# Query products as one block of 64x64 quarters behind the second stage's first product, and block sums over alternate tiles

## The chip, the cores and the metric

The kernel runs on one core of one Trainium2 chip. The metric is the device time of one launch in microseconds (us). A core has TensorE for matrix products (PE in the profile; PEld is its loading of weights), VectorE (DVE), ScalarE (ACT), GpSimd (POOL) and SyncE (SP), each of which works through its own instructions in program order and waits on the others' semaphores; DMA queues move data beside them.

## The reference

Linear attention over 8 batches, 8 heads, 576 tokens and head size 64, then an MLP with a residual over the 512 joined features:

```python
q_s = softmax(q, over the 64 features)      # exp, divided by its sum
k_s = softmax(k, over the 576 tokens)
kv  = einsum('bhsd,bhse->bhde', k_s, v)     # one 64x64 matrix a head
x   = einsum('bhsd,bhde->bhse', q_s, kv)    # joined to [8, 576, 512]
xn  = (x - mean) / sqrt(var + 1e-6) * g_ln
out = x + maximum(xn @ w_ch1, 0) @ w_ch2    # 512 -> 2048 -> 512
```

## The kernel before

The first 512 tokens of each batch are four tiles of 128 tokens. They make one turn of the MLP, and the last 64 tokens of all eight batches make a ninth turn of the same size (the code's `C9`, turn 8 when they are counted from 0, as here). Turns 2 to 8 are alike; turns 0 and 1 are special. Turn c runs the MLP of its tokens while the attention of turn c+1 and the loads and exponentials of turn c+2 are woven in between.

**The order.** Nothing schedules itself here. `mlp_steps(c)` gives a list of matmuls, the main line, each with a weight; a 256-column matmul weighs 0.5. A turn's list is 112 long: 0 to 56 is the first stage (features 512 to 2048), 56 to 112 the second (2048 to 512). `run` goes through that list and emits each side item when the sum of the weights reaches its number. So a side item such as `(10, reduce_q)` says where in every engine's program order it stands, and an engine does its instructions in that order, even when a later one could start.

**Both stages have seven products instead of eight** (2x2 blocks, sums of blocks as operands). Their order is 1, 5, 6, 2, 7, 3, 4. In the first stage the work is done for groups 0 and 1 and then, 28 further on, for groups 2 and 3; these are called pair A and pair B here. In each pair, every product is four matmuls of 256 columns for one group and four for the other. With two groups of a pair as g and g':

- products 1, 6, 7 and 4 pile up in one bank of PSUM, `bx`; 5 and 3 in `bb`; 2 in `bc`.
- after product 6 VectorE adds `bx` and a copy of product 5 into `bb` (`add_5`, L773), for g and then for g'. Product 7 adds to the same `bx`, so TensorE starts it for a group only when that group's L773 has read `bx`. Product 3 adds to `bb`.
- after product 7 VectorE writes one quarter of the hidden layer from `bx` (`out_22`, L776), for g and g', and applies the maximum to both (L781). Product 4 adds to `bx` again, so it waits for that group's L776.
- ScalarE copies (L766, L770) and writes the other quarters through the maximum (L784).

The second stage takes sums of the hidden layer's blocks (`sum_h`, L572: four sums over each half of the hidden layer, VectorE), which are side items at 30, 33 and 41 for the first half; its fourth sum and those of the second half come at the second stage's first products. Its products lie in the banks `ba`, `bb`, `bc` and `be` (L589), and VectorE makes the output from them (L601).

**Attention of the next turn.** `reduce_q` (L218) sums the exponentials of q in two instructions of two tiles; `recip_q` (L858) inverts the sums. `kv_pairs` (L361) makes the kv matrices; for each pair of heads `kv_sb` holds a 128x128 matrix with two 64x64 blocks and zeros beside them. `po_mm` (L404) multiplies: 16 matmuls of 128 columns a turn, woven in one by one, four of them to a tile. `x_fast` (L449) scales the tile's result, with its sum, and `xn_out` (L429) centres it. `xn_T` (L267) transposes two tiles by DMA, issued by SP. `sum_x` (L259) takes four differences of blocks of the transposed tiles on GpSimd, each in two instructions; products 5, 6, 7 and 4 of the next turn read them. For the ninth turn `po_mm` has a form of its own (L395): 64x64 quarters, 32 in one block, because the halves of a tile belong to two batches.

**PSUM.** `att_ps` has two banks (kv and query products), `mm_ps` six (the products of both stages).

In before, turn c+1's two `reduce_q` stand at 81 and 91 of turn c-1 and `recip_q` at 2 of turn c; for turn 3 alone the sums stand at 4 and 12 of turn 2. The query products of turn c+1 stand at 13 to 24, 48 to 53, 57 to 59 and 65 to 67 of turn c.

Of the kernel before, what the change touches and what calls it, by code (L numbers as in the profile page):

```python
# [20 lines left out]
def kernel(  # L21
# [16 lines left out]
    nc = tc.nc  # L38
# [66 lines left out]
    def main_src(x, b, h0, hn):  # L105
        return x[b, h0 : h0 + hn, 0:SM, :].rearrange("h (p t) d -> p h (t d)", t=T)

    raws = {}
# [134 lines left out]

    def sum_x(c, i):

        if i == 0:
            tqs[c] = mlp.tile([P, 4, 2, 2, P], BF16, tag="tq", name="tq", bufs=1)
        (b11, b12), (b21, b22) = [
            [xnTs[c][:, 2 * half : 2 * half + 2, 2 * kh : 2 * kh + 2, :] for half in range(2)]
            for kh in range(2)  # L250
        ]
# [130 lines left out]
    pobox = {}  # L382

    def po_mm(c, t, i):


        if c == C9:
            if i == 0 and t % 2 == 0:
                pobox["q"] = [
                    att_ps.tile([P, 2, NP, D], FP32, tag="a", name="po") for _ in range(2)  # L390
                ]
            pobox[c, t] = pobox["q"]
            for m, tok in enumerate(halves):
                for half, hs in enumerate(halves):
                    nc.tensor.matmul(  # L395
                        pobox["q"][half][tok, t % 2, i, :], eqTs[c][hs, t, i, tok],
                        kv_sb[hs, 2 * t + m, i, hs], start=(t % 2 == 0 and i == 0), stop=True,
                        skip_group_check=True,
                    )
            return  # L400
        if i == 0:
            pool, tag = (mm_ps, "m") if c == 0 and t >= 2 else (att_ps, "a")
            pobox["p"] = pobox[c, t] = pool.tile([P, DM], FP32, tag=tag, name="po")
        nc.tensor.matmul(  # L404
            pobox["p"][:, i * P : i * P + P], eqTs[c][:, t, i, :], kv_sb[:, c, i, :],
            start=True, stop=True,
        )
# [25 lines left out]

    def x_fast(c, t):

        x, st, _, mv = xs[c]
        if c == C9:
            for half in range(2):
                nc.vector.scalar_tensor_tensor(
                    x[:, t].rearrange("p (i two d) -> p i two d", two=2, d=D)[:, :, half],  # L440
                    in0=pobox[c, t][half][:, t % 2], scalar=1.0,
                    in1=eqs[c][2][:, t].rearrange("p (i two) -> p i two", two=2)[:, :, half]
                    .to_broadcast([P, NP, D]),
                    op0=ALU.mult, op1=ALU.mult, accum_out=st[:, t, half : half + 1],
                )
            nc.vector.tensor_add(mv[:, t, 0:1], st[:, t, 0:1], st[:, t, 1:2])
            xn_out(c, t)
            return
        nc.vector.scalar_tensor_tensor(  # L449
            x[:, t].rearrange("p (h d) -> p h d", h=H),  # L450
            in0=pobox[c, t].rearrange("p (h d) -> p h d", h=H), scalar=1.0,
            in1=eqs[c][2][:, t].to_broadcast([P, H, D]), op0=ALU.mult, op1=ALU.mult,
            accum_out=mv[:, t, 0:1] if c else st[:, t, 0:1],
        )
        if c:
            xn_out(c, t)
# [163 lines left out]
    def last_products(product):  # L620
# [7 lines left out]
        def stt(t, col, src, add=None, c0=0, cn=DH2):  # L628
            cols = slice(DH2 * col, DH2 * col + DH2)
            cs = slice(c0, c0 + cn)  # L630
            add = xs[c][0][:, t, cols] if add is None else add
            nc.vector.scalar_tensor_tensor(
                part(t, col)[:, cs], in0=src[:, cs], scalar=rstds[c][:, t : t + 1],
                in1=add[:, cs], op0=ALU.mult, op1=ALU.add,
            )

        def store(t0, tn, col):
            cols = slice(DH2 * col, DH2 * col + DH2)
            for half, eng in enumerate((nc.sync, nc.scalar)):
                ps = slice(64 * half, 64 * half + 64)  # L640
                to = out[2 * t0 + half : 2 * (t0 + tn) - 1 + half : 2, SM:S, cols]
                eng.dma_start(to.transpose([1, 0, 2]), yl[ps, t0 : t0 + tn, cols])
# [32 lines left out]
    def mm2_fast(c):  # L675
# [30 lines left out]

        def ys(name, col, t0):
            return [lambda t=t: y_quarter(c, t0 + t, col, hbox[name][:, t]) for t in range(2)]

        def sums(*which):  # L710
            return [lambda g=g, i=i: sum_h(g, i) for g, i in which if g or c == FAST or i == 3 or c == B - 1 and i > 1]

        late = c in (FAST, B - 1)
        product(1, "a", first=True, cut=6, at={
# [10 lines left out]
            1: ys("e", 1, 0)[:1], 4: ys("e", 1, 0)[1:],  # L725
            7: ys("b", 1, 2)[:1], 10: ys("b", 1, 2)[1:], 15: ys("a", 0, 2)})
        return steps

    def prod1(n, g, dst, c, q, ko, first):
# [7 lines left out]
        if n in (1, 2, 3):  # L737
            t0, kh = {1: (0, 0), 2: (0, 1), 3: (2, 1)}[n]
            rhs = xnTs[c][:, t0 : t0 + 2, 2 * kh + ko, :]
        else:  # L740
# [108 lines left out]
    def prep_fast(b):  # L849

        s = [(57, lambda: exp_q(b, 0, 4)), (65, lambda: exp_q(b, 2, 4)), (70, lambda: eq_T(b))]
        s += [(81, lambda: reduce_q(b, 0, 2)), (91, lambda: reduce_q(b, 2, 2))]
        s += [(81, lambda: exp_k(b, 0, 4)), (98, lambda: exp_k(b, 2, 4))]
# [6 lines left out]
    def attn_fast(c):  # L860

        s = [(4 + 4 * t, lambda t=t: reduce_q(3, t, 2)) for t in (0, 2)] if c == 3 else []
        kv, new, ps, squares, ts, rstd = (
            (24, 40, ((48, 53), (57, 59), (65, 67), (73, 75)), (66, 74, 87, 91), (61, 78), 95)
            if c == 3 else
            (3, 10, ((13, 24), (48, 53), (57, 59), (65, 67)), (60, 66, 74, 87), (55, 70), 92)
        )
        s += [(22 if c == 3 else 2, lambda: recip_q(c)), (kv, lambda: kv_pairs(c)), (new, lambda: start_x(c))]
        for t, (p0, p1) in enumerate(ps):
            s += spread([lambda t=t, i=i: po_mm(c, t, i) for i in range(NP)], p0, p1)  # L870
            s += [(p1, lambda t=t: x_fast(c, t)), (squares[t], lambda t=t: square_sum(c, t))]
        s += [(ts[0], lambda: xn_T(c, 0, 2)), (ts[1], lambda: xn_T(c, 2, 2)), (rstd, lambda: rstd_op(c))]
        s += [((84, 100 if c == C9 - 1 else 88, 92, 101)[i], lambda i=i: sum_x(c, i)) for i in range(4)]
        return s

    def second_side():
# [14 lines left out]
        s += [(40, lambda: start_x(2))]  # L891
        for t, (p0, p1) in enumerate(((47, 49), (51, 54), (57, 61), (65, 69))):
            s += spread([lambda t=t, i=i: po_mm(2, t, i) for i in range(NP)], p0, p1)
            s += [(p1, lambda t=t: x_fast(2, t)), ((69, 78, 84, 90)[t], lambda t=t: square_sum(2, t))]
# [3 lines left out]
        s += spread([lambda i=i: sum_x(2, i) for i in range(4)], 95, 108)  # L898
        return s

    def attn_rest():

        s = [(2, lambda: recip_q(C9)), (4, lambda: start_x(C9))]
        for t, (p0, p1, p2) in enumerate(((8, 21, 57), (8, 25, 62), (40, 52, 69), (40, 58, 77))):
            s += [(p0, lambda t=t: [po_mm(C9, t, i) for i in range(NP)])]
            s += [(p1, lambda t=t: x_fast(C9, t)), (p2, lambda t=t: square_sum(C9, t))]
        s += [(27, lambda: xn_T(C9, 0, 2)), (60, lambda: xn_T(C9, 2, 2)), (88, lambda: rstd_op(C9))]
        return s + spread([lambda i=i: sum_x(C9, i) for i in range(4)], 94, 102)

# [172 lines left out]
    with tc.manual_schedule(  # L1082
# [51 lines left out]
        for c in range(1, B):  # L1134
# [3 lines left out]
            else:  # L1138
                if c + 1 < B:
                    side += attn_fast(c + 1)  # L1140
                else:
                    side += attn_rest()
                if c + 2 < B:
# [3 lines left out]
            if c == B - 2:  # L1147
                side += [(1, load_qrem)]
                side += spread([lambda r=r: exp_qrem(r) for r in range(T)], 58, 80)
                side += [(84, lambda: eq_T(C9))]  # L1150
                side += [(84 + 4 * t, lambda t=t: reduce_q(C9, t, 2)) for t in (0, 2)]
            sums = [(53, 0)] if c == FAST else [(p, i) for i, p in enumerate((30, 41) if c == B - 1 else (30, 33, 41))]
            run(mlp_steps(c), side + [(at, lambda i=i: sum_h(0, i)) for at, i in sums])
# [31 lines left out]
```

## Time and profile before

| | before |
|---|---|
| median of 3 runs | 264.61 us (262.91 to 264.71) |
| the profiled execution | 263.19 us |
| its span, first to last instruction | 261.4 us |
| TensorE busy | 255.1 us, 98%, 2667 matmuls |
| VectorE busy | 223.9 us, 86% |
| ScalarE busy | 176.7 us, 68% |
| GpSimd busy | 94.4 us, 36% |
| granted TensorE clock | 0.999 |

The profile is one execution, whose own time lies 1.4 us under the median. TensorE's busy time is the time from a matmul's start to its modelled end, and the matmuls overlap, so the starts tell more than the ends: a 256-column matmul starts 0.109 us after the one ahead of it when nothing holds it up. VectorE's instructions overlap by some 0.08 us as well; what one of them costs the next is the distance between their starts.

### The profile page before, as it was taken

How to read it: one execution, taken by the hardware profiler on the slowest of the kernel's cores; microseconds unless marked ns; L12 is line 12 of the kernel's file. 1: busy time of each engine (PE TensorE's matmuls, PEld its weight loads, DVE VectorE, ACT ScalarE, POOL GpSimd, SP SyncE). 2: the span in 40 equal slices, each digit the busy share in tenths (PEclk: the TensorE clock that was granted, in tenths of full speed). 3: DMA queues.
4: the chain of work that ended last, by engine and by line, in shares of the span. 5: the costliest groups of instructions: out<-in, count | busy, mean ns of one | idle time of the engine just before them, and what ended most of it. 6: DMA issues, size and time to landing. Idle time of an engine off the chain costs nothing.

```text
span 261.4 us, 6802 instructions
## 1 busy us (share of the span) xinstructions
PE 255.1 (98%) x2667; PEld 219.9 (84%) x2667; DVE 223.9 (86%) x505; ACT 176.7 (68%) x348; POOL 94.4 (36%) x148
## 2 busy tenths in 40 slices
PE   8899999999999999999999999999999999999993
PEld 6789755788888998899889889988898888888883
DVE  6778996989999999899889988998898979977873
ACT  4657780997887785789478947894789277538400
POOL 3962228414059205920881088009100800030000
PEclk9999999999999999999999999999999999999999
DMA  7999999989999994999399938995905323221014
GB/s 195 253 206 207 356 215 276 290 192 285 171 143 277 274 174 33 294 264 115 84 263 263 154 79 290 245 153 130 266 4 111 112 102 44 43 104 56 3 41 120
DMA packets 82616, 45.00 MB, mean 172 GB/s; under 512 B 58196, under 2 KB 79192, under 8 KB 82584
## 3 DMA queue, kind: packets, MB, share of 16 engines
q0 software_dynamic: 32464, 21.76, 44.9%
q1 hardware_dynamic: 49488, 22.29, 40.6%
q10 hardware_dynamic: 632, 0.53, 0.7%
q8 instruction: 20, 0.33, 0.5%
q14 instruction: 12, 0.10, 0.1%
HBM read 36.70 MB, written 9.44 MB: 177 GB/s over the span
## 4 chain that ended last, share of the span: by engine, by line
PE 92%; DMA 3%; DVE 2%; SPq 1%; ACT 0%; issue 0%
PE ba L589 21%; PE bx L742 20%; PE bb L742 10%; PE ph L505 8%; PE bb L589 5%; PE bc L589 5%; PE be L589 5%; PE pc L541 5%; PE bc L742 5%; PE po L404 3%; DMA kt<-in_k_dram 3%; PE pkv L361 2%; PE ptr L918 1%; PE pxT L332 1%; SPq L970 1%; DVE bb L773 0%
## 5 line engine op out<-in xcount | busy, mean ns | idle before, releaser
L589 PEld LDWEIGHTS <-hs 128*128 128x128 bf16 x512 | 49.8, 98 | 5.8
L742 PEld LDWEIGHTS <-w_raw 128*128 128x128 bf16 x480 | 45.5, 98 | 5.2
L259 POOL TENSOR_TENSOR tq<-xnT 128x256 bf16<-128x256 bf16 x26 | 16.8, 665 | 73.7 <-DMA xnT<-xn 49.5
L589 PEld LDWEIGHTS <-hT 128*128 128x128 bf16 x392 | 37.4, 98 | 4.2
L742 PEld LDWEIGHTS <-w1g 128*128 128x128 bf16 x360 | 34.3, 98 | 4.3 <-issue 0.3
L742 PE MATMUL bx<-tq,w_raw 128*128 128x256 bf16 x240 | 31.6, 273 | 0.0
L589 PE MATMUL ba<-w_q,hs 128*128 128x256 bf16 x256 | 30.8, 273 | 0.0
L766 ACT COPY bc<-bx 128x512 f32<-128x512 f32 x30 | 16.6, 594 | 19.0 <-PE bx L742 19.0
L773 DVE TENSOR_TENSOR bb<-bx,s 128x512 f32<-128x512 f32 x30 | 19.5, 694 | 8.2 <-ACT s L770 5.5
L607 POOL DMA_DIRECT2D out_dram<-ot x28 | 15.5, 559 | 23.7 <-DVE ot L601 23.6
L784 ACT ACTIVATE hT<-bb 128x512 bf16<-128x512 f32 x30 | 16.3, 595 | 10.8 <-PE bb L742 10.8
L417 ACT ACTIVATE scrap<-x,mv 128x512 bf16<-128x512 bf16 x32 | 23.1, 722 | 0.3
L784 ACT ACTIVATE hT<-bc 128x512 bf16<-128x512 f32 x30 | 16.3, 594 | 8.9 <-PE bc L742 8.9
L572 DVE TENSOR_TENSOR hs<-hT 128x1024 bf16<-128x1024 bf16 x32 | 21.7, 685 | 0.5 <-ACT hT L784 0.5
L404 PE MATMUL po<-kv_sb,eqT 128*128 128x128 bf16 x128 | 22.0, 219 | 0.0
L776 DVE TENSOR_TENSOR hT<-bx,s 128x512 bf16<-128x512 f32 x30 | 19.3, 683 | 3.1 <-PE bx L742 3.1
L449 DVE SCALAR_TENSOR_TENSOR x<-po,rq 128x512 bf16<-128x512 f32 x30 | 20.5, 683 | 0.9 <-PE po L404 0.8
L218 DVE TENSOR_REDUCE zq<-eq 128x16 f32<-128x1024 bf16 (+1 forms) x20 | 20.8, 1050 | 0.5 <-ACT eq L209 0.5
L615 ACT COPY s<-ba 128x512 f32<-128x512 f32 x15 | 8.8, 585 | 14.7 <-PE ba L589 9.7
L784 ACT ACTIVATE hT<-bx 128x512 bf16<-128x512 f32 x30 | 16.4, 602 | 0.7 <-PE bx L742 0.6
L589 PE MATMUL ba<-w_sb,hT 128*128 128x256 bf16 x128 | 16.6, 273 | 0.0
L770 ACT COPY s<-bb 128x512 f32<-128x512 f32 x30 | 16.6, 622 | 0.0
(157 smaller groups left out, 553.5 us busy)
## 6 DMA issues: line engine op xcount, KB each, us to landing
out_dram<-ot POOLq DMA_DIRECT2D x30, 256.0 KB, 6.4
kt<-in_k_dram SPq DMA_DIRECT2D x5, 1024.0 KB, 12.3
qt<-in_q_dram SPq DMA_DIRECT2D x4, 1024.0 KB, 5.9
qt<-in_q_dram POOLq DMA_DIRECT2D x2, 1024.0 KB, 12.5
kt<-in_k_dram POOLq DMA_DIRECT2D x2, 1024.0 KB, 13.7
vm<-in_v_dram POOLq DMA_DIRECT2D x16, 128.0 KB, 11.1
qt<-in_q_dram SPq DMA_DIRECT2D x3, 512.0 KB, 4.7
w_raw<-in_moe_w_ch_dram POOLq DMA_DIRECT2D x3, 512.0 KB, 10.3
```

Of the source, the lines that this page charges most:

```text
L218: nc.vector.reduce_sum(eqs[c][1][:, ts], eqs[c][0][:, ts], axis=AX.X)
L259: eng.tensor_tensor(out=dst[:, t], in0=x[:, t], in1=y[:, t], op=ALU.subtract)
L404: nc.tensor.matmul(pobox["p"][:, i * P : i * P + P], eqTs[c][:, t, i, :], kv_sb[:, c, i, :], start=True, stop=True,)
L417: nc.scalar.activation(scrap, x[:, t], AF.Square, bias=mv[:, t, 0:1], scale=-float(DM), accum_out=mv[:, t, 1:2],)
L449: nc.vector.scalar_tensor_tensor(x[:, t].rearrange("p (h d) -> p h d", h=H), in0=pobox[c, t].rearrange("p (h d) -> p h d", h=H), scalar=1. ...
L505: nc.tensor.matmul(ph[:, m % 2, at : at + tn], (w1g if c else w1_sb)[:, ko, m * P : (m + 1) * P], xnTs[c][:, t0 : t0 + tn, ko, :], start=( ...
L572: nc.vector.tensor_tensor(out=dst, in0=x, in1=y, op=op)
L589: nc.tensor.matmul(hbox[bank][:, t, cs], lhsT, rhs[:, cs], start=first and (own or t == 0) and k == 0, stop=k == KH - 1, skip_group_check= ...
L742: nc.tensor.matmul(dst[:, q], lhsT, rhs, start=first and q == 0 and ko == 0, stop=ko == 1, skip_group_check=True)
L773: nc.vector.tensor_tensor(out=at[g, "b"], in0=at[g, "x"], in1=at[g, "s"], op=ALU.add)
L776: nc.vector.tensor_tensor(out=h_out(g, 1, 1), in0=at[g, "x"], in1=at[g, "s"], op=ALU.add)
L784: nc.scalar.activation(h_out(g, odd, half), at[g, name], AF.Relu)
```

## The change

1. **Query products.** For turns 3 to 8 the 16 woven matmuls become one block (`po_block`) of 64 quarters of 64x64: only the blocks of `kv_sb` that aren't zero are multiplied. It stands at 64, behind the second stage's first product. It writes two banks of `att_ps` for tiles 0 and 1 and two of `mm_ps` for tiles 2 and 3. Turn 8 has it in place of its two blocks of 32.
2. **What reads them.** `x_pair` replaces `x_fast`: for two tiles, four scalings of 256 columns, one add for the two sums, two centrings. Both pairs stand at 64, and so do the two transposes (64.1 and 64.3).
3. **Sums of exponentials.** The two `reduce_q` move from 81 and 91 of the turn before to 10 and 26 of this turn, `recip_q` from 2 to 40.
4. **Alternate tiles.** The halves of the tokens that the seven products work on were tiles 0, 1 and 2, 3; they are now tiles 0, 2 and 1, 3 (not for turns 0 and 1). One instruction of a `sum_x` then needs the first transpose alone and the other the second; the four first ones stand at 84, the four others at 88, all on GpSimd (VectorE did turn 8's eight and two of turn 7's).
5. **Sums of the hidden layer.** The fourth `sum_h` of the first half moves from the second stage (product 6) to 45. Turn 7, which had only two there (30 and 41), gets the same four places.
6. **Turn 1.** Its `x_fast` for tile 0 moves from 49 to 52.6, so behind L776 and L781 of its pair; tile 3's query product moves from 65..69 to 62..65; tiles 2 and 3 take banks of `mm_ps`; `sum_x` stands at 88 and 94.

```diff
+    def paired(c):
+        return c > 1
+    def half_tiles(c, half):
+        return slice(half, T, 2) if paired(c) else slice(2 * half, 2 * half + 2)
...
+    def sum_x(c, i, ts=range(2)):
...
-        eng = nc.vector if c == C9 or (c == C9 - 1 and i == 1) else nc.gpsimd
-        for t in range(2):
-            eng.tensor_tensor(out=dst[:, t], in0=x[:, t], in1=y[:, t], op=ALU.subtract)
+        for t in ts:
+            nc.gpsimd.tensor_tensor(out=dst[:, t], in0=x[:, t], in1=y[:, t], op=ALU.subtract)
...
+    def po_block(c):
+        for t0, pool, tag in ((0, att_ps, "a"), (2, mm_ps, "m")):
+            banks = [pool.tile([P, 2, NP, D], FP32, tag=tag, name="po") for _ in halves]
+            for t in range(2):
+                pobox[c, t0 + t] = [bank[:, t] for bank in banks]
+                for i in range(NP):
+                    for m, tok in enumerate(halves):
+                        for bank, hs in zip(banks, halves):
+                            nc.tensor.matmul(
+                                bank[tok, t, i, :], eqTs[c][hs, t0 + t, i, tok],
+                                kv_sb[hs, 2 * (t0 + t) + m if c == C9 else c, i, hs],
+                                start=(t == 0 and i == 0), stop=True, skip_group_check=True,
+                            )
...
+    def x_pair(c, t0):
+        x, st, _, mv = xs[c]
+        for t in (t0, t0 + 1):
             for half in range(2):
                 nc.vector.scalar_tensor_tensor(
...
+        ts = slice(t0, t0 + 2)
+        nc.vector.tensor_add(mv[:, ts, 0:1], st[:, ts, 0:1], st[:, ts, 1:2])
+        for t in (t0, t0 + 1):
             xn_out(c, t)
...
     def attn_fast(c):
-        s = [(4 + 4 * t, lambda t=t: reduce_q(3, t, 2)) for t in (0, 2)] if c == 3 else []
...
+        s = [(at, lambda t=t: reduce_q(c, t, 2)) for t, at in ((0, 10), (2, 26))]
+        s += [(40, lambda: recip_q(c))]
+        if c < C9:
+            s += [(24 if c == 3 else 3, lambda: kv_pairs(c))]
+        s += [(60, lambda: start_x(c)), (64, lambda: po_block(c))]
+        s += [(64 + p, lambda t=t: x_pair(c, t)) for t, p in ((0, 0), (2, 0.2))]
+        s += [(64.1, lambda: xn_T(c, 0, 2)), (64.3, lambda: xn_T(c, 2, 2))]
+        s += [((72, 76, 80.5, 87)[t], lambda t=t: square_sum(c, t)) for t in range(T)]
+        s += [(92, lambda: rstd_op(c))]
+        s += [(84 + 4 * t, lambda i=i, t=t: sum_x(c, i, (t,))) for t in range(2) for i in range(4)]
...
-            sums = [(53, 0)] if c == FAST else [(p, i) for i, p in enumerate((30, 41) if c == B - 1 else (30, 33, 41))]
+            sums = [(53, 0)] if c == FAST else [(p, i) for i, p in enumerate((30, 33, 41, 45))]
```

More of the change, by code (lines that the diff above doesn't have):

```diff
@@ L382 @@
     pobox = {}
-    def po_mm(c, t, i):
[L387 to L400, printed above, removed]
+    def po_block(c):
[11 more added lines that the diff above has]
+                            )
+    def po_mm(c, t, i):
         if i == 0:
-            pool, tag = (mm_ps, "m") if c == 0 and t >= 2 else (att_ps, "a")
+            pool, tag = (mm_ps, "m") if c in (0, 2) and t >= 2 else (att_ps, "a")
             pobox["p"] = pobox[c, t] = pool.tile([P, DM], FP32, tag=tag, name="po")
@@ L405, in po_mm @@
             pobox["p"][:, i * P : i * P + P], eqTs[c][:, t, i, :], kv_sb[:, c, i, :],
-            start=True, stop=True,
+            start=(i == 0), stop=True, skip_group_check=True,
         )
@@ L705, in mm2_fast, with ys @@
             return steps
-        def ys(name, col, t0):
-            return [lambda t=t: y_quarter(c, t0 + t, col, hbox[name][:, t]) for t in range(2)]
+        def ys(name, col, half):
+            return [
+                lambda t=t: y_quarter(c, tile_of(c, half, t), col, hbox[name][:, t])
+                for t in range(2)
+            ]
         def sums(*which):
-            return [lambda g=g, i=i: sum_h(g, i) for g, i in which if g or c == FAST or i == 3 or c == B - 1 and i > 1]
-        late = c in (FAST, B - 1)
+            return [lambda g=g, i=i: sum_h(g, i) for g, i in which if g or c == FAST]
+        late = c == FAST
         product(1, "a", first=True, cut=6, at={
```

59 lines of the change are left out of this document (18 added, 41 removed).

## The prediction

> **What bounds the kernel.** I read the chain of waits first. It is TensorE from end to end:
>
> ```profile
> PE 92%; DMA 3%; DVE 2%; SPq 1%; ACT 0%; issue 0%
> ```
>
> Then the timeline of TensorE within turn 4, whose first matmul starts at 128.66. All times below that have no trace time beside them count from such a first matmul.
>
> ```profile
> 131.27 1.04 PE L742 MATMUL bx<-tq,w_raw 128*128 128x256 bf16 x8
> 132.14 0.38 PE L742 MATMUL bc<-xnT,w1g 128*128 128x256 bf16 x2
> ...
> 133.13 0.71 PE L742 MATMUL bx<-tq,w_raw 128*128 128x256 bf16 x5
> ```
>
> Eight matmuls take 0.87 (131.27 to 132.14): 0.109 each, with no hole. A turn's 224 make 24.46; with the kv products (0.86 with what they cost at both ends) and 16 query products (0.055 each: 132.36 to 132.42 in the timeline) that is 26.2, which is what a turn takes (129.48 to 155.69 from one turn's kv products to the next's). So from turn 2 on TensorE never waits. The change can win only what it takes from TensorE's stream, and loses whatever wait it brings in. The candidate is VectorE, in the first stage, since TensorE there waits for it four times a pair (L773 and L776, each group). Its timeline in turn 4, where the last number of a row is the idle time ahead of it:
>
> ```profile
> 131.98 1.30 DVE L773 TENSOR_TENSOR bb<-bx,s 128x512 f32<-128x512 f32 x2 [0.63 <-PE bx L742]
> 133.76 1.29 DVE L776 TENSOR_TENSOR hT<-bx,s 128x512 bf16<-128x512 f32 x2 [0.49 <-PE bx L742]
> 135.09 0.43 DVE L781 TENSOR_SCALAR hT<-hT 128x1024 bf16<-128x1024 bf16 x1
> 135.43 0.68 DVE L449 SCALAR_TENSOR_TENSOR x<-po,rq 128x512 bf16<-128x512 f32 x1
> ...
> 138.33 1.30 DVE L773 TENSOR_TENSOR bb<-bx,s 128x512 f32<-128x512 f32 x2 [0.49 <-ACT s L770]
> 139.53 0.68 DVE L572 TENSOR_TENSOR hs<-hT 128x1024 bf16<-128x1024 bf16 x1
> 140.13 1.28 DVE L776 TENSOR_TENSOR hT<-bx,s 128x512 bf16<-128x512 f32 x2
> ```
>
> The pairs run without slack to speak of: the second L773 ends at 133.27 (4.61), and product 7 of that group, the fifth matmul of the row at 133.13, starts at 133.57: 0.30 later. What a late one costs, turn 1 shows (VectorE, then TensorE):
>
> ```profile
> 61.89 1.27 DVE L776 TENSOR_TENSOR hT<-bx,s 128x512 bf16<-128x512 f32 x2
> ```
> ```profile
> 61.81 0.71 PE L742 MATMUL bb<-xnT,w_raw 128*128 128x256 bf16 x5
> 62.62 0.38 PE L742 MATMUL bx<-tq,w1g 128*128 128x256 bf16 x2
> ```
>
> Five matmuls from 61.81 are through at 62.36; product 4 starts at 62.62, 0.05 after the first L776 ends (62.56). So a wait is paid in full, plus 0.05.
>
> **Query products.** The form is in the trace, in turn 7:
>
> ```profile
> 208.16 1.04 PE L742 MATMUL bb<-tq,w_raw 128*128 128x256 bf16 x8
> 209.13 0.45 PE L395 MATMUL po<-kv_sb,eqT 64*64 64x64 bf16 x32
> 209.51 1.05 PE L742 MATMUL bx<-tq,w_raw 128*128 128x256 bf16 x8
> ```
>
> The eight matmuls are through at 209.03, the next start at 209.51: 0.48 for 32 quarters. 0.09 is lost ahead (209.03 to 209.13); by the single starts four quarters follow each other every 0.032, so eight fours are 0.25, and the remaining 0.13 is lost at the first four and behind. A block of 64 pays this once: 16 x 0.032 + 0.22 = 0.72, against 16 x 0.055 = 0.88. That is -0.16 in each of turns 2 to 6 and 2 x 0.48 - 0.72 = -0.24 in turn 7: **-1.0**. Four banks in place of two are not in the trace; bounds are nothing saved and the quarters at a quarter of a whole matmul's time (rival D). The Trainium skill (TensorEngine Tiling, Theoretical Speedup) promises up to 2x for each small dimension, 4x for both; its Key Properties say that a change of tiling mode drains the engine. The 0.09 is that drain. The 4x does not hold here: 0.032 against 0.055 is 1.7x. By 4x the block would be 0.44, and the gain 2.7 in place of 1.0.
>
> **The sums of exponentials.** One `reduce_q` costs VectorE 1.13: in turn 2, where before has one between L773 and L776, it starts at 79.88 and the next at 81.01.
>
> ```profile
> 78.68 1.30 DVE L773 TENSOR_TENSOR bb<-bx,s 128x512 f32<-128x512 f32 x2 [0.22 <-ACT s L770]
> 79.88 1.21 DVE L218 TENSOR_REDUCE zq<-eq 128x16 f32<-128x1024 bf16 x1
> 81.01 1.28 DVE L776 TENSOR_TENSOR hT<-bx,s 128x512 bf16<-128x512 f32 x2
> ```
>
> There it fills a hole, because kv stands at 24 in that turn and holds TensorE back. At 10 it comes *between the two L773*: product 6 of group 0 ends with 9.5, that of group 1 with 11.5. Queued behind it are the second L773 and, on TensorE, product 7 of group 1.
>
> *Pair A, turns 3 to 6.* First L773 3.32 (131.98), reduce 0.60 later, second L773 another 1.13 later, 0.69 long: it ends at 5.74. TensorE would start product 7 of group 1 at 0.86 + 18 x 0.2184 = 4.79 (the woven products are gone); it starts at 5.79. **1.00 lost.** Product 7 then ends at 6.23, the second L776 runs 6.42 to 7.11 (0.19 behind, as at 133.76), product 4 of that group starts at 7.54 and doesn't wait. L781 7.14 to 7.57.
>
> *Pair B.* Second reduce from 7.50, next start 8.63: the first two block sums 8.63 to 10.04 (0.69 and 0.04 each). TensorE's product 6 is through at 7.97 + 2.18 = 10.15; first L773 at 10.43, second 11.03 to 11.72: in time for product 7 (11.90). Then `recip_q` (0.26), the third sum and, new here, the fourth, which ends at 13.31; the first L776 starts at 13.22 instead of 12.1 and ends at 13.91. Product 4 could start at 7.97 + 24 x 0.2184 = 13.21 and starts at 13.96: 0.75. The second L776 ends at 14.50: another 0.15. **0.90 lost.** What left this stretch, one L449 with its L429 (1.00), and its idle 0.49 twice, are less than what came: 2.26 + 0.26 + 0.72.
>
> That is 1.90 in each of turns 3 to 6. Turn 2 (kv at 24): 1.00, 0.09 at the second L773 of pair B, since kv's three VectorE steps (0.95) now stand ahead of the second reduce, 1.04 at L776: 2.13. Turn 7 (no kv): 1.00 + 0.91. Sum: 7.6 + 2.1 + 1.9 = **+11.6**.
>
> **The second stage** I cost at nothing; the covers are these. `x_pair`: by turn 7's L439 rows four scalings 0.34 apart, add and two centrings come to 2.2, twice 4.4 against 4.0 before. TensorE passes the block at 16.7 to 17.5; the pairs run 17.3 to 21.65, the last block sum and the seed of `be` behind them until 22.9, and product 3 needs that at 24.4: 1.5 of cover. If VectorE were later by more, the excess would be paid each turn. Transposes: the second is ready to go at 21.65, lands 4.2 later by the median (3.1 to 8.2), at 25.9; the turn ends at 27.9: 2.0 of cover. GpSimd's eight differences (0.63 each) end at some 28.8, each ahead of its product (the first 26.9 for 29.7). Turn 8's eight, now on GpSimd too, have the same cover, about 2. Banks: the block takes the attention's own two and two whose last use was `bb` of pair B, free from some 14 on, 2.7 ahead of the block.
>
> **Turn 1.** With `x_fast` behind L776 the wait at 62.62 goes (0.26) and one of 0.05 behind it: -0.3. Its other hole (0.11, second L773) stays.
>
> **Sum:** -1.0 + 11.6 - 0.3 = +10.3. On the profiled execution's 263.2 that is 273.5; on the median, 264.6, 274.9. I forecast the middle: **274.2 us**.
>
> **The rivals.**
> A. *The stalls don't come (not slower).* It decides at one point: if the second L773 ends by 4.74, TensorE doesn't wait. For it: VectorE has 0.63 idle just ahead of the first L773, and the reduce's data are there long before. Against: the program order, and turn 2's reduce, which held L776 back until 81.01 although `bx` was ready. Then 264.6 - 1.3 = 263.3. Chance 0.12, of which 0.03 for over 1% faster.
> B. *Only pair A stalls.* For it: behind the first stall ScalarE and VectorE are ahead of TensorE, and my second stall rests on a longer sum. 6 x 1.0 - 1.3 = +4.7: 269.3. Chance 0.15.
> C. *The transposes come late.* Two of them now go off close together with the next turn's q behind them; at the row's longest, 8.2, the turn's first product waits 1.9 more: 6 x 1.9 = +11: 285.6. Against: their longest is one of 14. Chance 0.07.
> D. *Quarters at a quarter of a whole matmul's time:* 16 x 0.055 / 4 + 0.22 = 0.44 a block, 2.7 saved in all: the forecast less 1.7, 272.5. Against: the starts in turn 7. The skill's 4x (above) is this rival. Chance 0.03.
> The forecast keeps 0.63.
>
> **Range.** 268.5 to 279.5: down to B, up by the cover of `x_pair` failing by 0.8 in six turns; A and C, 0.19, stay outside. 1% (2.6 us) is about what a measurement of this kernel can tell from no change (its three runs lie 1.8 apart). Faster 0.03, same 0.09, slower 0.88.
>
> **What would show it.** Right: TensorE's starts in turns 2 to 7 with a hole of 1.0 ahead of the fifth matmul of pair A's product 7, ended by that group's L773, and of 0.75 ahead of pair B's product 4; turns of some 27.9; L218 between two L773. Block of 64 in 0.72. Wrong: turns of 26.0 without holes (A), holes ahead of a turn's first product (C) or of product 3 in the second stage (the cover of `x_pair`).

## The result and the profile after

| | before | changed |
|---|---|---|
| median of 4 runs | 264.56 us (262.91 to 264.71) | 275.06 us (273.79 to 276.46) |
| the profiled execution: time, span | 263.19, 261.4 us | 275.58, 273.5 us |
| TensorE busy | 255.1 us, 98% | 257.3 us, 94% |
| VectorE busy | 223.9 us, 86% | 224.9 us, 82% |

The changed kernel is slower: the ratio is 1.041, with a 95% interval of 1.035 to 1.048. Of the experiments' runs below, one fell into a slower state of the chip and is left out of the numbers. The engines do almost the same work as before. Line numbers have moved: L773, L776, L781, L572, L218 and L858 on VectorE are L791, L794, L799, L585, L227 and L875 now, L742 and L589 on TensorE are L760 and L602, and the block of query products is L401.

In the changed kernel's chain of waits, TensorE's share has fallen from 92% to 66%:

```profile
PE 66%; DVE 16%; ACT 6%; DMA 5%; issue 4%; SPq 1%; DVEq 0%; ACTq 0%
```

Its costliest groups (busy time, mean, then idle time of the engine just before them and what ended it). In before the first of these rows had no idle at all:

```profile
L760 PE MATMUL bx<-tq,w_raw 128*128 128x256 bf16 x240 | 32.4, 272 | 5.5 <-DVE bb L791 5.5
...
L760 PE MATMUL bx<-tq,w1g 128*128 128x256 bf16 x120 | 16.7, 272 | 2.6 <-DVE hT L794 2.6
```

So TensorE waits for the two VectorE steps L791 and L794. Where they come late is in the timeline of VectorE in turn 5, whose first matmul starts at 161.92:

```profile
165.24 0.70 DVE L791 TENSOR_TENSOR bb<-bx,s 128x512 f32<-128x512 f32 x1 [0.63 <-PE bx L760]
165.97 1.22 DVE L227 TENSOR_REDUCE zq<-eq 128x16 f32<-128x1024 bf16 x1
167.11 0.69 DVE L791 TENSOR_TENSOR bb<-bx,s 128x512 f32<-128x512 f32 x1
...
172.54 1.30 DVE L791 TENSOR_TENSOR bb<-bx,s 128x512 f32<-128x512 f32 x2 [0.45 <-ACT s L788]
173.75 0.34 DVE L875 RECIPROCAL rq<-zq 128x32 f32<-128x32 f32 x1
174.01 0.63 DVE L585 TENSOR_TENSOR hs<-hT 128x1024 bf16<-128x1024 bf16 x1
174.55 0.68 DVE L585 TENSOR_TENSOR hs<-hT,hs 128x1024 bf16<-128x1024 bf16 x1
175.15 1.28 DVE L794 TENSOR_TENSOR hT<-bx,s 128x512 bf16<-128x512 f32 x2
```

and in TensorE's of the same turn:

```profile
166.28 0.60 PE L760 MATMUL bx<-tq,w_raw 128*128 128x256 bf16 x4
167.85 0.60 PE L760 MATMUL bx<-tq,w_raw 128*128 128x256 bf16 x4 [0.97 <-DVE bb L791]
...
174.40 1.04 PE L760 MATMUL bb<-xnT,w_raw 128*128 128x256 bf16 x8
175.89 1.20 PE L760 MATMUL bx<-tq,w1g 128*128 128x256 bf16 x8 [0.45 <-DVE hT L794]
...
178.76 0.74 PE L401 MATMUL po<-kv_sb,eqT 64*64 64x64 bf16 x64
179.43 1.92 PE L602 MATMUL bb<-w_q,hs 128*128 128x256 bf16 x16
```

The reduction stands between the two L791. The second of them starts at 167.11; without the reduction it would follow the first by 0.60, as in before, and start at 165.84, which is 1.27 earlier. So product 7 of the second group, which could go on at 166.28 + 4 x 0.109 = 166.72, starts at 167.85: a hole of 1.13. In pair B the reciprocal and two block sums stand between L791 and L794. Product 4 starts 0.62 late (174.40 + 8 x 0.109 = 175.27, against 175.89) and loses another 0.17 within its eight matmuls, when it reaches the second group. Taken so from TensorE's starts, the holes of the profiled execution are:

| turn | ahead of pair A's product 7 | pair B's product 4 | others | sum | forecast |
|---|---|---|---|---|---|
| 2 | 0.99 | 0.69 + 0.16 | 0.15 + 0.16 in pair B, 0.11 at product 5 | 2.26 | 2.13 |
| 3 to 6, each | 1.13 | 0.57 to 0.62, + 0.17 | | 1.87 to 1.92 | 1.90 |
| 7 | 0.99 | 0.57 + 0.16 | | 1.72 | 1.91 |

They sum to 11.5. The profiled execution has one hole more, 1.55 ahead of turn 2's first product, which the last experiments look at. A turn (3 to 6) takes 27.94 to 28.00, against 26.21 before.

### The profile page after: what moved, and what is told of

Same layout as the page of the kernel before. It is cut to its first block, busy times and chain, and to the rows that moved or that the text cites. A ratio compares the mean times of both kernels' runs of the same rounds, so it can differ in the third digit from the quotient of the medians.

```text
span 273.5 us, 7325 instructions
## 1 busy us (share of the span) xinstructions
PE 257.3 (94%) x2904; PEld 218.1 (80%) x2907; DVE 224.9 (82%) x543; ACT 179.1 (65%) x348; POOL 100.8 (37%) x158
## 4 chain that ended last, share of the span: by engine, by line
PE 66%; DVE 16%; ACT 6%; DMA 5%; issue 4%; SPq 1%; DVEq 0%; ACTq 0%
PE ba L602 18%; PE bx L760 11%; PE ph L518 7%; PE pc L554 5%; PE bb L602 5%; DVE bb L791 5%; PE bc L602 4%; PE be L602 4%; PE bb L760 4%; DVE hs L585 3%; DMA xnT<-xn 3%; DVE zq L227 3%; DMA kt<-in_k_dram 2%; ACT hT L802 2%; ACT bc L784 2%
## 5 line engine op out<-in xcount | busy, mean ns | idle before, releaser
L267 POOL TENSOR_TENSOR tq<-xnT 128x256 bf16<-128x256 bf16 x30 | 20.0, 669 | 108.1 <-PE bc L602 78.5
L760 PEld LDWEIGHTS <-w_raw 128*128 128x128 bf16 x480 | 46.6, 98 | 12.5 <-issue 6.9
L602 PEld LDWEIGHTS <-hs 128*128 128x128 bf16 x512 | 49.6, 98 | 6.0
L760 PEld LDWEIGHTS <-w1g 128*128 128x128 bf16 x360 | 34.5, 98 | 10.4 <-issue 6.3
L602 PEld LDWEIGHTS <-hT 128*128 128x128 bf16 x392 | 37.6, 98 | 4.2
L760 PE MATMUL bx<-tq,w_raw 128*128 128x256 bf16 x240 | 32.4, 272 | 5.5 <-DVE bb L791 5.5
L602 PE MATMUL ba<-w_q,hs 128*128 128x256 bf16 x256 | 30.6, 273 | 0.0
L791 DVE TENSOR_TENSOR bb<-bx,s 128x512 f32<-128x512 f32 x30 | 20.0, 694 | 11.4 <-ACT s L788 8.9
L585 DVE TENSOR_TENSOR hs<-hT 128x1024 bf16<-128x1024 bf16 x32 | 21.4, 675 | 1.1 <-ACT hT L802 0.5
L227 DVE TENSOR_REDUCE zq<-eq 128x16 f32<-128x1024 bf16 (+1 forms) x20 | 20.8, 1053 | 0.7 <-ACT eq L218 0.5
L794 DVE TENSOR_TENSOR hT<-bx,s 128x512 bf16<-128x512 f32 x30 | 19.8, 684 | 1.5 <-PE bx L760 0.8
L267 POOL TENSOR_TENSOR tq<-xnT,tq 128x256 bf16<-128x256 bf16 x30 | 20.0, 669 | 1.1
L760 PE MATMUL bx<-tq,w1g 128*128 128x256 bf16 x120 | 16.7, 272 | 2.6 <-DVE hT L794 2.6
L802 ACT ACTIVATE hT<-bx 128x512 bf16<-128x512 f32 x30 | 17.0, 603 | 2.9 <-PE bx L760 2.9
L447 DVE SCALAR_TENSOR_TENSOR x<-po,rq 128x256 bf16<-128x256 f32 x48 | 17.5, 420 | 1.4 <-PE po L401 1.4
L760 PE MATMUL bx<-xnT,w1g 128*128 128x256 bf16 x120 | 16.2, 273 | 1.4 <-DMA xnT<-xn 1.4
L760 PE MATMUL bc<-xnT,w1g 128*128 128x256 bf16 x120 | 15.7, 273 | 0.0
```

What stands on the lines that cost most here:

```text
L227: nc.vector.reduce_sum(eqs[c][1][:, ts], eqs[c][0][:, ts], axis=AX.X)
L267: nc.gpsimd.tensor_tensor(out=dst[:, t], in0=x[:, t], in1=y[:, t], op=ALU.subtract)
L447: nc.vector.scalar_tensor_tensor(x[:, t].rearrange("p (i two d) -> p i two d", two=2, d=D)[:, :, half], in0=pobox[c, t][half], scalar=1.0, ...
L585: nc.vector.tensor_tensor(out=dst, in0=x, in1=y, op=op)
L602: nc.tensor.matmul(hbox[bank][:, t, cs], lhsT, rhs[:, cs], start=first and (own or t == 0) and k == 0, stop=k == KH - 1, skip_group_check= ...
L760: nc.tensor.matmul(dst[:, q], lhsT, rhs, start=first and q == 0 and ko == 0, stop=ko == 1, skip_group_check=True)
```

## The experiments

The theory: TensorE loses what stands in VectorE's program order between two steps that it waits for, at the length of what stands there; the quarters' block, the pairs of scalings and the transposes cost nothing that shows. The main rival: the block, its four banks or the late transposes make the loss, and the holes are where it happens to show. The first four kernels ran beside 263.61 us (262.93 to 265.28) for before.

### One reduction moved by one step

```diff
-        s = [(at, lambda t=t: reduce_q(c, t, 2)) for t, at in ((0, 10), (2, 26))]
+        s = [(at, lambda t=t: reduce_q(c, t, 2)) for t, at in ((0, 12), (2, 26))]
```

> The changed kernel with the first sum of exponentials of q at 12 instead of 10, so behind the second L791 (the add into bb) of pair A instead of ahead of it; nothing else. Theory (the order on VectorE makes the holes): the hole of 1.0 to 1.13 us ahead of the second group's product 7 goes; what is left is that the writes from bx (L794) come later: some 0.44 a turn in turns 3 to 6 and 7, nothing in turn 2, where the kv products stand in between. 4 x 0.7 + 1.0 + 0.55 = 4.3 us faster than the changed kernel, 270.7 us. Rival (the block of quarters, x_pair or the transposes behind it make the loss): 275 us, unchanged.

Measured: 271.03 us (270.42 to 271.70), 1.028 of before (1.024 to 1.032). VectorE in turn 5 of this kernel:

```profile
161.60 1.30 DVE L791 TENSOR_TENSOR bb<-bx,s 128x512 f32<-128x512 f32 x2 [0.63 <-PE bx L760]
162.93 1.22 DVE L227 TENSOR_REDUCE zq<-eq 128x16 f32<-128x1024 bf16 x1
164.07 1.28 DVE L794 TENSOR_TENSOR hT<-bx,s 128x512 bf16<-128x512 f32 x2
```

Both L791 are together now (x2), and the hole ahead of product 7 is gone. In its place there is, in turns 3 to 6, 0.42 + 0.15 ahead of product 4, since L794 now waits behind the reduction, but with the length of product 3 as cover: while VectorE is late, TensorE still has that product to do. Pair A's holes fall from 6.5 us in six turns (0.99 + 4 x 1.13 + 0.99) to 2.7 (4 x 0.57 + 0.42), for one instruction moved by one step. Little moves elsewhere: the hole ahead of pair B's product 7 in turn 2 grows from 0.15 to 0.37.

### The fourth block sum taken back

```diff
-            return [lambda g=g, i=i: sum_h(g, i) for g, i in which if g or c == FAST]
+            return [lambda g=g, i=i: sum_h(g, i) for g, i in which if g or c == FAST or i == 3]
...
-            sums = [(53, 0)] if c == FAST else [(p, i) for i, p in enumerate((30, 33, 41, 45))]
+            sums = [(53, 0)] if c == FAST else [(p, i) for i, p in enumerate((30, 33, 41))]
```

> The changed kernel with the fourth block sum of the first half back behind the second stage's product 6, as in before; nothing else. Theory: the holes at pair B's product 4 (0.57 and 0.16 a turn) shrink to some 0.2, those of pair A stay: 6 x 0.53 = 3.2 us faster than the changed kernel, 271.9 us. Rival (it is the second reduce and recip_q in pair B that fill VectorE, and the sum only moves the hole to the second stage): 274 to 275 us.

Measured: 271.38 us (271.03 to 272.01), 1.029 (1.025 to 1.033). Pair A's hole stays at 1.13 in each of turns 3 to 6; pair B's shrink from 0.57 + 0.16 to 0.13 (0.16 in turn 5), in turn 2 from 0.69 + 0.16 to 0.09 + 0.16. So that sum, 0.60 long, is what makes most of pair B's hole; without it the second reduction and the reciprocal nearly fit in.

### Reductions and reciprocal taken back

```diff
+        s += [(81, lambda: reduce_q(b, 0, 2)), (91, lambda: reduce_q(b, 2, 2))]
...
-        s = [(at, lambda t=t: reduce_q(c, t, 2)) for t, at in ((0, 10), (2, 26))]
-        s += [(40, lambda: recip_q(c))]
+        s = [(4 + 4 * t, lambda t=t: reduce_q(3, t, 2)) for t in (0, 2)] if c == 3 else []
+        s += [(22 if c == 3 else 2, lambda: recip_q(c))]
...
+                side += [(84 + 4 * t, lambda t=t: reduce_q(C9, t, 2)) for t in (0, 2)]
```

> The changed kernel with the sums of exponentials and recip_q where before has them (81 and 91 of the turn before, 2 of this turn); block, x_pair, alternate tiles and the fourth block sum at 45 as changed. Theory: pair A has no hole; pair B keeps some 0.6 from the fourth block sum; the second stage holds the reduces, since x_pair leaves 1.5 us of cover there: 6 x 0.6 - 1.1 = 2.8 us over before, 267.4 us. If the second stage's cover fails instead: 0.7 a turn more, 271 to 272 us. Rival (block and transposes make the loss): 275 us.

Measured: 266.09 us (265.23 to 267.01), 1.009 (1.007 to 1.012). No hole is left at pair A's product 7; pair B has 0.37 + 0.16 (0.43 + 0.16 in turn 5), the fourth sum alone; turn 2 has 0.43 at product 5. The block of quarters, the pairs and the transposes are all still in this kernel, which is 2.5 us over before. What they cost together, less what the quarters and turn 1 save, is at most what those 2.5 leave beside pair B's holes; six times 0.53 is 3.2, so nothing is left. The main rival falls.

### Only the reductions moved, in the kernel before

```diff
-        s += [(81, lambda: reduce_q(b, 0, 2)), (91, lambda: reduce_q(b, 2, 2))]
...
-        s = [(4 + 4 * t, lambda t=t: reduce_q(3, t, 2)) for t in (0, 2)] if c == 3 else []
+        s = [(at, lambda t=t: reduce_q(c, t, 2)) for t, at in ((0, 4 if c == 3 else 10), (2, 12 if c == 3 else 20))]
...
-        s += [(22 if c == 3 else 2, lambda: recip_q(c)), (kv, lambda: kv_pairs(c)), (new, lambda: start_x(c))]
+        s += [(22, lambda: recip_q(c)), (kv, lambda: kv_pairs(c)), (new, lambda: start_x(c))]
```

> The kernel before with the sums of exponentials moved into the turn that needs them in turns 3 to 6 (to 10 and 20, recip_q to 22); no block, nothing else of the change. Theory: the second L773 of pair A ends 1.13 us later, a hole of 0.9 ahead of the second group's product 7, and some 0.5 in pair B: 1.4 in each of four turns, 5.6 us over before, 270.2 us. Rival (VectorE has 0.6 us idle ahead of each pair and takes them up): 264.6 to 265 us.

Measured: 271.71 us (271.04 to 272.59), 1.029 (1.024 to 1.034). VectorE, then TensorE, in turn 5 of this kernel, whose lines are before's:

```profile
163.73 0.70 DVE L773 TENSOR_TENSOR bb<-bx,s 128x512 f32<-128x512 f32 x1 [0.63 <-PE bx L742]
164.46 1.22 DVE L218 TENSOR_REDUCE zq<-eq 128x16 f32<-128x1024 bf16 x1
165.60 0.69 DVE L773 TENSOR_TENSOR bb<-bx,s 128x512 f32<-128x512 f32 x1
```
```profile
166.34 0.27 PE L742 MATMUL bx<-tq,w_raw 128*128 128x256 bf16 x1 [0.86 <-DVE bb L773]
...
172.89 1.20 PE L742 MATMUL bx<-tq,w_raw 128*128 128x256 bf16 x8 [0.60 <-DVE bb L773]
```

Holes of 1.02 in pair A and, here ahead of pair B's product 7, of 0.76 to 0.98 + 0.16, with nothing of the rest of the change. They sum to 8.0, and the kernel is 8.1 slower than before, though the move touches four turns only; the theory had 5.6, with 0.5 in pair B. So moving reductions makes such holes without the rest of the change. The 8.1 is not a share of the changed kernel's 10.5: here the second reduction stands at 20, with the reciprocal and one tile's scaling (L449) behind it, and pair B's hole is at another product.

### Both late additions taken back: a cover runs out

The third experiment's edit and the second's together.

> The changed kernel with both late additions to VectorE's first stage taken back: the reductions and their reciprocal where the kernel before has them (second stage and the front of the next turn), the fourth block sum back at product 6. The block of quarters, the scaling in pairs, the alternate tiles and turn 1 stay changed. Theory: no hole is left in the first stage; the reductions alone left 0.37 + 0.16 in pair B of six turns (3.2), so 266.1 - 3.2 = 262.9, against 263.6 for the kernel before: a ratio of 0.997 (0.993 to 1.001). Rival (the block, its two banks more or the close transposes cost something of their own, hidden so far behind the holes): 265 to 266, with new holes in front of product 3 of the second stage or of a turn's first product.

Measured: 264.70 us (264.10 to 266.00) beside 263.83 (262.94 to 266.01) for before, as for the three kernels after it: 1.004 (1.001 to 1.006), not the 0.997 of the theory. The holes in both pairs are gone, and there is a new one of 0.36 in each of turns 2 to 5, ahead of the second stage's product 3 (besides 0.24 ahead of product 5 in turn 2 and 0.40 ahead of and in product 5 of turn 7). VectorE and TensorE there, in turn 3 of this kernel:

```profile
122.47 1.29 DVE L585 TENSOR_TENSOR hs<-hT,hs 128x1024 bf16<-128x1024 bf16 x2
123.68 1.21 DVE L227 TENSOR_REDUCE zq<-eq 128x16 f32<-128x1024 bf16 x1
124.80 0.69 DVE L631 TENSOR_TENSOR be<-bb,s 128x512 f32<-128x512 f32 x1
```
```profile
123.44 1.91 PE L602 MATMUL ba<-w_q,hs 128*128 128x256 bf16 x16
125.55 1.91 PE L602 MATMUL be<-w_sb,hs 128*128 128x256 bf16 x16 [0.20 <-DVE be L631]
```

Product 3 could start at 123.44 + 16 x 0.109 = 125.19; the seed of its bank (L631, the add from which the bank starts) ends at 125.49. Behind the block, VectorE has the scalings in pairs (4.45), two block sums (1.2), a reduction (1.13) and this seed, and that is 0.36 too long. In the changed kernel the reduction and one of the two sums are elsewhere, and the seed ends early; in turn 5:

```profile
184.31 0.69 DVE L631 TENSOR_TENSOR be<-bb,s 128x512 f32<-128x512 f32 x1
```

That is 1.43 ahead of product 3 (186.43): 1.43 + 0.36 is 1.79, those two within 0.06. With the reduction there and one sum (the third experiment), it ends 0.29 early (177.93 + 0.69, against 178.91). So the pairs are hidden only while at least one of the two additions to the first stage stays out of the second: parts of the change that could be taken for independent share one cover.

### Whole products in place of the quarters

```diff
-        s += [(60, lambda: start_x(c)), (64, lambda: po_block(c))]
-        s += [(64 + p, lambda t=t: x_pair(c, t)) for t, p in ((0, 0), (2, 0.2))]
+        s += [(60, lambda: start_x(c)), (64, lambda: whole_block(c))]
+        s += [(64 + p, lambda t=t: x_two(c, t)) for t, p in ((0, 0), (2, 0.2))]
```

on the kernel with both additions back. Here `whole_block` is 16 `po_mm` in a row, tiles 2 and 3 in banks of `mm_ps`, and `x_two` is two `x_fast`, but for turn 7, where they are `po_block` and `x_pair`.

> As the one before (both late additions taken back), but the block of batches 3 to 7 is made of 16 whole products with four whole scalings, as the kernel before computes them, in the same place; only the block of turn 7 stays in quarters. Theory: a block of quarters is 0.76 in the trace of the changed kernel, 16 whole products are 0.88: five blocks, 0.6 slower than the one before, so 263.5. Rival (quarters are worth nothing, since the change of tiling mode is paid at both ends): the same time to 0.2. VectorE's work per block is 0.4 less, which should show nowhere.

Measured: 264.15 us (263.49 to 265.35), 1.002 (1.000 to 1.004): 0.55 less than with quarters by the medians, though the intervals overlap, and not the 0.6 more of the theory. The block itself is as the theory has it. TensorE in turn 3 of this kernel (query products are L427 here, the second stage L617):

```profile
116.72 1.06 PE L427 MATMUL po<-kv_sb,eqT 128*128 128x128 bf16 x16
117.61 1.91 PE L617 MATMUL bb<-w_q,hs 128*128 128x256 bf16 x16
```

Sixteen whole products take 0.89; the 64 quarters take 0.67 from their first to the next product (178.76 to 179.43 above), and 0.09 are lost ahead of them: 0.76. Ahead of the whole products nothing is lost: the matmul in front of them starts at 116.61, 0.109 earlier. But "VectorE's work is 0.4 less, which should show nowhere" was wrong: four whole scalings and their centrings take 4.0 here, the pairs 4.45 (118.02 to 122.47 in the experiment before), and they start 0.47 ahead of the block's end instead of 0.17 (117.14 against 117.61, 118.02 against 118.19). With 0.75 more of cover the 0.36 hole is gone. Turns 3 to 5 take 26.21 each here and 26.45 with quarters.

### Turn 2 in the old order

```diff
     def paired(c):
-        return c > 1
+        return c > 2
```

on the kernel with both additions back.

> As the first of these three, but batch 2's tiles stay in their old halves (0,1 and 2,3); from batch 3 on they alternate. Theory: the hole at the start of turn 2 (1.55 in the profiled execution of the changed kernel, 0.24 to 0.33 in three of the experiments) comes from the alternate tiles: product 1 of turn 2 then needs both transposes of turn 1, and its differences both, where the kernel before needed only the first; without it TensorE has no hole there and the time is 0.3 less than the first of these three (262.6). Rival (the loads in flight or the order of turn 1 hold it): the hole stays, the time is the same.

Measured: 265.94 us in five runs (265.14 to 267.00), 1.008 (1.005 to 1.012): 1.2 slower than the kernel it was made from, neither theory nor rival. GpSimd and TensorE at the start of turn 2:

```profile
76.54 0.67 POOL L267 TENSOR_TENSOR tq<-xnT 128x256 bf16<-128x256 bf16 x1 [14.05 <-DMA xnT<-xn]
```
```profile
76.03 1.04 PE L760 MATMUL bx<-xnT,w1g 128*128 128x256 bf16 x8
79.88 0.38 PE L760 MATMUL bb<-tq,w_raw 128*128 128x256 bf16 x2 [2.82 <-POOL tq L267]
```

Product 1 starts without a wait, as the theory had it, but product 5 waits 2.98. With tiles 0, 1 and 2, 3 as halves, every difference needs both transposes, so GpSimd starts at 76.54 instead of 73.58, and the fifth difference, the second half of what product 5 reads, ends only at 79.83. Not all of the 2.98 is the order's. The profiled execution is the slowest of the five, and its second transpose landed 7.2 after its issue, against 5.3 in the kernel with both additions back: some 2 us of the hole are that, by estimate, and the 1 us that is left is of the size of the 1.2 between the medians. The alternate tiles make product 1 wait for the second transpose, but they let GpSimd start on the first, and with the differences in this order that is worth more. (Before had in-order tiles too, but took each difference for both tile pairs at once, so that product 5 needed the first two only; GpSimd started at 74.56.)

### The reduction ahead of the kv products

```diff
-        s = [(at, lambda t=t: reduce_q(c, t, 2)) for t, at in ((0, 10), (2, 26))]
-        s += [(40, lambda: recip_q(c))]
+        s = [(at, lambda t=t: reduce_q(c, t, 2)) for t, at in ((0, 1), (2, 26))]
+        s += [(57, lambda: recip_q(c))]
```

on the changed kernel, with the fourth block sum back at product 6.

> The changed kernel with its reductions left in the first stage of the turn that uses them, but at other places: the first at 1, ahead of the kv products, in VectorE's idle time there (0.53 and 0.63), the second at 26 as it is, the reciprocal behind pair B, the fourth block sum back at product 6. Theory (it is the place between two dependent steps that makes the holes, not the stage or the amount): no hole in pair A, at most 0.15 in pair B; 262.9 to 263.8. Rival (VectorE's first stage is simply full, so that 2.3 more of it always delay TensorE): holes of 0.5 to 1 in each of six turns, 266 to 270.

Measured: 263.11 us (262.52 to 264.42), 0.998 (0.996 to 1.001): the rival falls. VectorE in turn 4 of this kernel:

```profile
129.77 1.21 DVE L227 TENSOR_REDUCE zq<-eq 128x16 f32<-128x1024 bf16 x1
...
132.09 1.30 DVE L791 TENSOR_TENSOR bb<-bx,s 128x512 f32<-128x512 f32 x2
133.76 1.29 DVE L794 TENSOR_TENSOR hT<-bx,s 128x512 bf16<-128x512 f32 x2 [0.38 <-PE bx L760]
```

The same two reductions, in the same stage of the same turn, make no hole in turns 3 to 7. The first one takes the idle time that VectorE had there, and the second stands behind pair A's last L794. VectorE is not too full for the reductions; their places were wrong. The fourth sum is not in the first stage of this kernel, but neither is it in the second experiment's, which differs from this one only in the places of the first reduction and the reciprocal and has 1.13 in pair A of turns 3 to 6 (1.029 of before). The second stage has no hole either: without a reduction there, the seed of product 3 ends 0.76 early, 1.13 less the 0.36. A turn takes 26.09: 0.12 less than before's 26.21, which is the quarters' gain.

### Turn 2 too

The kernel before this one, edited further:

```diff
-        s = [(at, lambda t=t: reduce_q(c, t, 2)) for t, at in ((0, 1), (2, 26))]
+        s = [(at, lambda t=t: reduce_q(c, t, 2)) for t, at in (((0, 4), (2, 12)) if c == 3 else ((0, 1), (2, 26)))]
...
-        s += [(88 + 6 * t, lambda i=i, t=t: sum_x(2, i, (t,))) for t in range(2) for i in range(4)]
+        s += [(88 + 6 * t + 6 * (i // 2), lambda i=i, t=t: sum_x(2, i, (t,))) for i0 in (0, 2) for t in range(2) for i in (i0, i0 + 1)]
```

> As the kernel with the reduction ahead of the kv products, and in turn 2 alone: the reductions where the kernel before has them there (between the first pair's two groups of steps, at 4 and 12, where TensorE is held back less), and GpSimd's differences of batch 2 ordered so that both tile pairs of the first two differences come ahead of the others. Theory: the holes that are left in turn 2 (0.24 ahead of product 5, where the fifth difference ends last, and 0.15 + 0.16 in pair B) go, 0.55 in all; 0.9979 of the kernel before by holes alone becomes 0.996, about 262.6. Rival (the difference waits for the second transpose, not for its turn on GpSimd): the 0.24 stays, 262.8 to 263.

Measured: 262.58 us (262.03 to 264.14) beside 263.76 (262.50 to 264.74) for before: 0.9965 (0.9942 to 0.9987). Its median is the lowest of all kernels here, and it is faster than before by 0.1 to 0.6%; its interval overlaps that of the kernel before this one. Its chain of waits:

```profile
PE 92%; DMA 4%; POOL 2%; DVE 1%; issue 0%; DVEq 0%
```

From turn 2 on TensorE has no hole left; turns 2 to 6 take 26.09 each and turn 7 25.23. The 0.24 ahead of product 5 was GpSimd's order, not the transpose: the difference that product 5 waits for is now the third and ends at 75.98, where as the fifth it ended at 77.07, 0.05 ahead of product 5.

### The changed kernel again

> The changed kernel once more, nothing edited: whether the hole of 1.55 at the start of turn 2, which the profiled execution showed and no experiment since, belongs to the change. Theory (the two transposes took 3.9 each to issue and landed late in that execution; elsewhere 2.5): a hole of 0.24 to 0.33 ahead of product 5 in its place, the other holes as before, a span near 272.3. Rival (it belongs to the change): 1.5 again, a span near 273.5.

Measured: 273.72 us (273.36 and 274.08) beside 263.76 for before, span 272.0. The hole at the start of turn 2 is 0.25, ahead of product 5; all others are within 0.02 of the table above. So the 1.55 doesn't come with every execution of the change: where it came, the two transposes took 7.99 to issue and landed 9.7 and 8.0 after it, here 6.21, landing after 7.8 and 5.0. That a late second transpose can hold up product 1 is the alternate tiles' doing; why they were late then is not known.

## Why the prediction was right

The forecast was 274.2 and the sum +10.3; the medians lie 10.5 apart. By its steps:

- **TensorE never waits from turn 2 on, so every hole is paid in full.** Right. The changed kernel again has 11.4 of holes in turns 2 to 7 without the one of product 5, and its turns are longer by just their holes less the quarters' gain (27.95 - 26.21 = 1.74 in turn 3, against 1.87 - 0.12 = 1.75).
- **Query products, -1.0.** A block was forecast at 0.72 and takes 0.76: 0.12 a turn in place of 0.16, and 0.19 in place of 0.24 in turn 7 (25.42 to 25.23 in the last version). -0.8 in all. The groups of four follow each other every 0.032, as forecast. The mis-sized term is what the block loses beside them: 0.22 was forecast (0.09 ahead, 0.13 at the first four and behind, and 0.51 + 0.22 is 0.73 rather than 0.72), and it is 0.09 + 0.16 = 0.25. The Trainium skill (TensorEngine Tiling (Array Packing), Theoretical Speedup) gives up to 2x for each small dimension. Here 16 whole products against the 64 quarters are 0.89 against 0.67, 1.3x, and with the 0.09 ahead of them 0.89 against 0.76, 1.2x. Rival D had 0.44 a block and falls by the 0.76. That the 0.09 is a change of tiling mode is not shown by an edit, but fits: kv's products, 128x64, have 0.09 ahead of them too, and the whole products of the sixth experiment have nothing.
- **Pair A, 1.00.** Measured 0.99 in turns 2 and 7, but 1.13 in turns 3 to 6. The term that was off there is the 0.60 from the first L791 to the reduction: it is 0.73. In turn 2 of before a reduction starts 0.10 ahead of the end of its L773, here it starts 0.03 behind the end (165.24 + 0.70, then 165.97). The traces show a pattern: a reduction straight behind this add starts 0.03 behind its end wherever VectorE's last write to SBUF ahead of the add was kv's (L377, 64 partitions), in turns 3 to 6 of five profiles, and 0.09 ahead of it in the fifteen other places. No edit tests whether that write is the cause. What the reduction costs the next, 1.13, was right (1.14).
- **Pair B, 0.75 + 0.15.** Measured 0.57 to 0.62, + 0.17. The first L794's end, which is what TensorE waits for, was forecast for 13.91 after the turn's start and is at 13.91 (175.83). It is TensorE that was later, by pair A's extra 0.13: the same end, less to wait. That the end is the same is luck: VectorE's pair B begins 0.19 later than forecast (172.54 is 10.62, against 10.43), and the third and fourth sums take 1.14 (174.01 to 175.15), not the 1.33 of the forecast, whose fourth sum was priced at 0.72 and takes 0.60. So the errors cancel, 1.90 against 1.87 to 1.92 a turn. In turn 7, forecast as the others without kv, pair B's is 0.19 under (0.57 against 0.76). That the fourth sum makes this hole (rival B's doubt) is shown by the second and third experiments.
- **The second stage at nothing.** Right for the changed kernel, with a cover of 1.4 against 1.5. But that cover is made by the other parts: with the reductions and the fourth sum in their old places the same chain is 0.36 late, which the prediction's "if VectorE were later by more" named without seeing that the change itself had paid for it.
- **Transposes and GpSimd.** Right for turns 3 to 7. For turn 2 the forecast saw no hole at product 5: it is 0.11 to 0.25, from GpSimd's order. Rival C's wait came in one place of one profiled execution, 1.55 ahead of turn 2's first product, instead of six times 1.9. It wasn't the rival's mechanism: turn 1's transposes stand where they stood, and it is the alternate tiles that make product 1 need the second one. The close transposes of turns 2 to 7 held nothing up in the changed kernel.
- **Turn 1, -0.3.** The holes of 0.26 and 0.05 are gone, the 0.11 stays, and a new 0.06 stands in its second stage.
- **Rival A** would have needed the reduction to run in VectorE's idle time. It needs an edit for that, and the kernels with the reduction ahead of kv are that edit, with the fourth sum back as well: 263.1 and 262.6, where the rival said 263.3.

So: -0.8 + 11.5 - 0.3 = +10.4, against 10.5 between the medians. The profiled spans lie 12.1 apart (273.5 - 261.4), close to the 10.4 and the 1.55, and with the second profile of the changed kernel, without the 1.55, 10.6 (272.0). The mechanism was right; that the sum came so near is in part luck, since pair A's holes (6.5, forecast 6.0) and the others (5.0, forecast 5.6) were off in opposite ways.

The Trainium skill (PSUM — Partial Sum Buffer, Engine vs sequencer instructions) says that VectorE's queue is "strict FIFO". The trace agrees: the second L791 had its data (TensorE was past product 6 at 165.41, ScalarE past its copies at 165.42) and stood 1.14 behind a reduction that nothing needed before the reciprocal in pair B.

## What to carry to other kernels

On an engine that another one waits for several times in a row, an instruction costs what its place makes it cost: the same 1.13 us reduction, once in each of six turns, cost 6.5 us between two steps that TensorE waits for, 2.7 one step later, and nothing in turns 3 to 7 where the engine had been idle anyway. (These are sums of holes.) Before moving work, list the idle gaps of the engine that receives it and put the work into one, and check the cover that it leaves behind as well as the one that it takes. Parts of a change that look independent can share one cover, so undo them together as well as one by one.

## What was not expected of the hardware

- Quarters gain little: a block of 64 of them takes 0.76 (0.67 and 0.09 lost ahead) where 16 whole products take 0.88, though it leaves out the half of the multiplications that meets zeros.
- The same two DMA transposes, in the same place of the same kernel, took 7.99 to issue and 8.0 to 9.7 to land in one execution, 6.21 and 5.0 to 7.8 in another.
- A reduction behind an add of VectorE starts 0.10 ahead of the add's end in some places (turn 2 of before: 78.68 + 1.30, then 79.88) and 0.03 behind it in others (turn 5 of the changed kernel: 165.94, then 165.97), which made a 0.13 error in each of four turns.
